# Two pairs of batch 2 move from TensorE to an elementwise local attention, and block 2's steps are reordered

## The chip, the cores and the metric

The kernel runs on one core of one Trainium2 chip. The metric is the device time of one execution in microseconds (us), the median of several runs; one further execution was taken by the hardware profiler. The engines are PE (TensorE, matrix products, with its weight loads counted apart as PEld), DVE (VectorE), ACT (ScalarE), POOL (GpSimd) and SP (SyncE, which here issues all DMAs). Each engine works through its own instructions strictly in order and waits on semaphores for the others. SBUF is the working memory with 128 partitions, PSUM the memory of 8 banks into which PE writes.

## The reference

The input q, k, v has 8 batches, 8 heads, 576 positions and 64 values per head. Two attentions are added and go through a feed-forward layer:

```python
q_d = q.reshape(B, H, Sd, 4, D).mean(axis=3)        # k_d, v_d alike; Sd = 144
out_up = np.repeat(sm_attn(q_d, k_d, v_d), 4, axis=2)
mask = np.abs(pos[:, None] - pos[None, :]) < 4       # 7 neighbours
attn = softmax(np.where(mask, scale * q @ k.T, -1e9))
x = (out_up + attn @ v).transpose(0, 2, 1, 3).reshape(B * S, H * D)   # 4608 x 512
r = np.maximum(x @ w_in, 0.0)                        # w_in 512 x 2048
out = (s * (r * r) + b) @ w_out                      # w_out 2048 x 512
```

All of it is float32.

## The kernel before

**Feed-forward.** The 4608 tokens are cut into 18 blocks of 256 (index t), and the 2048 hidden values into 8 f pairs of 256 (index p). A step (t, p) has a `gemm1` (lines 551 to 570: 24 matmuls into a PSUM tile `ph`, then relu, square and a rounded copy `gh` on ACT and the rest `gl` on DVE) and a `gemm2` (lines 586 to 616: 12 matmuls that add to two PSUM banks `po` of the block; at p = 7 the sums are scaled, given the bias and written out). Each float32 product is made from three products of rounded halves (lines 556 to 558 and 601 to 603). `gemm2` runs two or three steps behind `gemm1`, by the list `pend`. For t = 0 and t = 2 the tile `ph` is bank 4; t = 1 uses bank 7 up to p = 6 and bank 4 at p = 7; from t = 3 on, banks 4 and 6 take turns.

**Order of the steps** (lines 653 to 656): f pairs 0 to 6 for blocks 0 and 1 in turn, then f pairs 0 to 6 of block 2, then f pair 7 of blocks 0, 1 and 2, then block after block. The weights are converted meanwhile (`split_w`, lines 214 to 253): for f pairs 0 to 6 from staging tiles of 1024 elements, for f pair 7 from quarters of 256 (`load_quarter`, line 205), which are loaded into the tag `pv` with two buffers. The scratch tile `es` of this conversion is taken from `pv` for f pairs 0, 1 and 7, and from the tags `xl2` and `os` for the others. `add_rows` (line 572) adds the rows of w_out into `bias` on DVE, one f pair at each step from step 13 on, f pair 7 first; `column_sums` (line 581) makes the constant part of the output from it.

**Attention.** A unit is one pair of heads of one batch (pairs 0 to 3). The pooled attention (`down`, lines 268 to 342) uses PE, ACT, DVE and POOL alike in all units. The local attention has two forms. Batches 0, 1 and 2 (`first_unit`, lines 344 to 437) make scores in windows of 32 on PE (lines 383 and 388), a softmax on DVE and ACT, and the output again on PE (line 431). From batch 3 on, two pairs make a group (`local_unit`, lines 452 to 505): for each of 7 offsets POOL multiplies q by the shifted k (line 466) and DVE sums over the 64 values (468); after the softmax, for each offset DVE weights the shifted v (484, 487) and POOL or DVE adds (488). Nine transposes on PE (line 498) turn the sums, and DVE adds them into x (502). The scores `st` of a group stand in PSUM bank 7. `two_pairs` (line 511) weaves a group with the two pooled attentions that belong to it.

**Order of the attention.** `attention_rest` (line 664) yields a sequence of small pieces; after each step, `advance` emits pieces until a target is reached that grows for each batch from 0 at step `free[b]` to all its pieces (`NY[b]`) at step `need[b]`. The framework then orders each engine's instructions by priority and by a simulated timeline, so that pieces may run earlier or later than the step that emits them. `rings` gives the PSUM banks that the pieces of a batch take in turn: 5 and 6 for batch 1, 5 for the first two units of batch 2, and 2, 3 and 5 after that.

**Splits and buffers.** Before block t starts, `split_x` (line 529) needs the whole of the batches that it touches, and splits x into `xh` and `xl`; for block 2 in the tags `os` and `xl2` with one buffer each, for the others in `xh` and `xl` with two. Block 2 holds the end of batch 0 and the start of batch 1; block 4 the end of batch 1 and the start of batch 2. The output rows `os_` of every block stand in the tag `os`. The group's q and k (`lqk`) and v (`lv`) use the tags `big` and `vw`, one buffer each, which the units of `first_unit` use for `db` and `tvw`.

Of the kernel before, what the change touches and what calls it, by code (L numbers as in the profile page):

```python
# [11 lines left out]
F32 = mybir.dt.float32  # L12
F32R = mybir.dt.float32r
I32 = mybir.dt.int32
# [5 lines left out]
P = 128  # L20
B, H, S, D = 8, 8, 576, 64
HP = H // 2
FAC = 4
SD = S // FAC
DM = H * D
# [11 lines left out]
TB = 256  # L37
NB = NT // TB
NFP = DFF // 256
NK = DM // P  # L40
NE = 3
EU = NE * HP
CH = 9
NC_ = S // CH
HALO = FAC - 1
NO = 2 * HALO + 1
# [2 lines left out]

STAGE = (6, 6, 7, 6, 7, 6, 7)  # L50
CONVERT_AT = (1, 2, 4, 6, 7, 8, 11)
CHUNK = (512, 512, 512, 1024, 1024, 512, 1024)
BEHIND = {1: 400, 2: 100, 4: 100, 5: 400}
HF = 7
GROUPS = [(i // HP, i % HP // 2) for i in range(EU, B * HP, 2)]
# [7 lines left out]
def attention_ffn_kernel(ctx, tc, qk, vw_in, vr_in, vdm, qkn, vn, w_in, w_out, s_in, b_in, out):  # L63
    nc = tc.nc
# [3 lines left out]
    one = ctx.enter_context(tc.tile_pool(name="one", bufs=1))  # L68
    two = ctx.enter_context(tc.tile_pool(name="two", bufs=2))
    ps = ctx.enter_context(tc.tile_pool(name="ps", bufs=1, space=PS))  # L70

    def bank(i, shape, name):
        return ps.tile(shape, F32, tag=f"k{i}", name=name)
# [128 lines left out]
            nc.sync.dma_start(st.rearrange("p (k f) t -> p k (f t)", k=src.shape[1]), src)  # L202
            wst[(p, op)] = st

    def load_quarter(p, op, i):
        if op == "i":
            src = src_i[:, i, 512 * p : 512 * p + 512]
        else:
            src = src_o[:, 2 * p + i // 2, 512 * (i % 2) : 512 * (i % 2) + 512]
        st = two.tile([P, 256, 2], I32, tag="pv", name="wst")  # L210
        nc.sync.dma_start(st.rearrange("p f t -> p (f t)"), src)
        return st

    def convert(st, hi, lo, op, p):


        n = hi.shape[1]
        top, low = st[:, :, 1], st[:, :, 0]
        if p in (0, 1, 7):
            f = two.tile([P, n], F32, tag="pv", name="es")  # L220
        else:
            f = one.tile([P, n], F32, tag="xl2" if op == "i" else "os", name="es")
        w = f.bitcast(I32)


        nc.scalar.mul(f, top.bitcast(F32), 2.0 ** -112)
        nc.vector.tensor_scalar(f, f, W_MAX, -W_MAX, ALU.min, ALU.max)
        nc.vector.tensor_scalar(w, w, 3, 0x7FFFFFF8, ALU.logical_shift_left, ALU.bitwise_and)
        nc.vector.scalar_tensor_tensor(w, low, 29, w, ALU.logical_shift_right, ALU.bitwise_or)
        nc.vector.scalar_tensor_tensor(w, top, -0x80000000, w, ALU.bitwise_and, ALU.bitwise_or)  # L230
        nc.scalar.copy(hi, f)
        for i in range(0, n, 512):
            js = slice(i, min(i + 512, n))
            nc.vector.tensor_tensor(lo[:, js], f[:, js], hi.bitcast(F32)[:, js], ALU.subtract)
# [5 lines left out]
    def split_parts(p):  # L240
        wi[p] = one.tile([P, 2, NK, 256], F32R, tag=f"wi{p}", name="wi")
        wo[p] = one.tile([P, 2, 2, DM], F32R, tag=f"wo{p}", name="wo")
        for op, w in (("i", wi[p]), ("o", wo[p])):
            fl = w.rearrange("p s k f -> p s (k f)")
            if p < len(STAGE):
                st = wst.pop((p, op))
                for j in range(0, 1024, CHUNK[p]):
                    js = slice(j, j + CHUNK[p])
                    convert(st[:, js], fl[:, 0, js], fl[:, 1, js], op, p)
            else:  # L250
                for i in range(4):
                    cs = slice(256 * i, 256 * i + 256)
                    convert(load_quarter(p, op, i), fl[:, 0, cs], fl[:, 1, cs], op, p)


    xt = {}
# [195 lines left out]
    def local_unit(b, g, banks):  # L452

        acc = two.tile([P, CH, 2, D], F32, tag="qk", name="acc")

        st = bank(7, [P, 2, P], "st")
        for h in range(2):
            lqk = one.tile([P, 2 * CH + 2 * HALO, D], F32, tag="big", name="lqk")
            nc.sync.dma_start(lqk, qkn[GROUPS.index((b, g)), h])
            lv = one.tile([P, CH + 2 * HALO, D], F32, tag="vw", name="lv")  # L460
            nc.sync.dma_start(lv, vn[GROUPS.index((b, g)), h])
            ls = take(st[:, h], 0, [P, CH, NO])
            sums = st[:, h, 64 : 64 + CH]
            for o in range(NO):
                pr = two.tile([P, CH, D], F32, tag="pl", name="pr")
                nc.gpsimd.tensor_tensor(  # L466
                    pr, lqk[:, 0:CH], lqk[:, CH + o : 2 * CH + o], ALU.mult)
                nc.vector.tensor_reduce(ls[:, :, o], pr, AX.X, ALU.add)  # L468
                yield
            row = lambda t: t.unsqueeze(2).to_broadcast([P, CH, NO])  # L470
            nc.vector.tensor_tensor(ls, ls, omask, ALU.add)
            lr = two.tile([P, 2, CH], F32, tag="lr", name="lr")
            nc.vector.tensor_reduce(lr[:, 0], ls, AX.X, ALU.max)
            nc.vector.tensor_tensor(ls, ls, row(lr[:, 0]), ALU.subtract)
            nc.scalar.activation(ls, ls, AF.Exp, scale=SCALE)
            nc.vector.tensor_reduce(sums, ls, AX.X, ALU.add)
            nc.vector.tensor_scalar(sums, sums, 1e-9, None, ALU.add)
            nc.vector.reciprocal(lr[:, 1], sums)
            nc.vector.tensor_tensor(ls, ls, row(lr[:, 1]), ALU.mult)
            yield  # L480
            for o in range(NO):
                w = ls[:, :, o : o + 1].to_broadcast([P, CH, D])
                if o == 0:
                    nc.vector.tensor_tensor(acc[:, :, h], lv[:, 0:CH], w, ALU.mult)
                else:
                    pv = two.tile([P, CH, D], F32, tag="pv", name="pv")
                    nc.vector.tensor_tensor(pv, lv[:, o : o + CH], w, ALU.mult)  # L487
                    (nc.vector if o % 3 == 1 else nc.gpsimd).tensor_tensor(  # L488
                        acc[:, :, h], acc[:, :, h], pv, ALU.add)
                yield  # L490
        yield "ready"
        x = xt[b]
        for i0 in range(0, CH, 4):
            n = min(4, CH - i0)
            ot = banks([P, n, P], "ot")
            with tc.high_priority():
                for j in range(n):
                    nc.tensor.transpose(
                        ot[:, j], acc[:, i0 + j].rearrange("p h d -> p (h d)"), ident)
            for u in range(2):  # L500
                xv = x[:, 2 * g + u].rearrange("p (c i) -> p c i", i=CH)[:, :, i0 : i0 + n]
                nc.vector.tensor_tensor(
                    xv, ot[:, :, 64 * u : 64 * u + 64].rearrange("p j c -> p c j"), xv, ALU.add)
            yield
        complete.update((b, 2 * g + u) for u in range(2))
# [5 lines left out]
    def two_pairs(b, g, banks):  # L511
        for u in range(2):
            load_pair(b, 2 * g + u)
        dn = chain(*(down_unit(b, 2 * g + u, banks) for u in range(2)))
        lo = local_unit(b, g, banks)
        i = 0
        for said in lo:
            if said == "ready":
                for _ in dn:
                    yield  # L520
            elif i % 3 == 2:
                next(dn, None)
            i += 1
            yield
# [22 lines left out]

    gt = {}
    oacc = {}

    def gemm1(t, p):
        xh, xl = xs[t]
# [33 lines left out]
    def gemm2(t, p):  # L586
# [5 lines left out]
            oacc[t] = [bank(i, [P, DM], "po") for i in ob]  # L592
        po = oacc[t]
        end = t == NB - 1 and p == NFP - 1
        os_ = one.tile([P, 2, DM], F32, tag="os", name="os") if p == NFP - 1 else None
        for m in range(2):
            ms = slice(P * m, P * m + P)
            for j in range(2):
# [22 lines left out]
    def banks(*ids):  # L621
        ring = itertools.cycle(ids)
        return lambda shape, name: bank(next(ring), shape, name)
# [2 lines left out]
        for j in range(i, min(i + 3, EU)):  # L626
            load_pair(*units[j])

    NY = [10 * HP] * NE + [34 * (HP // 2)] * (B - NE)
    for hp in range(2, HP):  # L630
        load_pair(0, hp)
    load_w(0)
# [18 lines left out]


    order = [(t, p) for p in range(HF) for t in range(2)]
    order += [(2, p) for p in range(HF)]
    order += [(t, p) for p in range(HF, NFP) for t in range(3)]
    order += [(t, p) for t in range(3, NB) for p in range(NFP)]

    need = [0, 2 * HF - 3] + [(S * b // TB) * NFP - 3 for b in range(2, B)]
    free = [0, 0, 16] + [((S * (b - 1) - 1) // TB) * NFP - 2 for b in range(3, B)]


    rings = {1: banks(5, 6), 2: banks(5), 3: banks(2, 3, 5)}

    def attention_rest():
        for i in range(HP, EU):
            load_ahead(i)
            yield from first_unit(*units[i], rings[min(i // HP + i // (EU - 2), 3)])
        for b, g in GROUPS:
            yield from two_pairs(b, g, rings[3])

    gen = attention_rest()
    done = 0
    pend = []

    def target(st):
        return sum(
            min(1.0, max(0.0, (st - free[b]) / (need[b] - free[b]))) * NY[b]
            for b in range(1, B))

    def advance(st):  # L680
        nonlocal done
# [88 lines left out]
```

## Time and profile before

| what | us |
|---|---|
| median of 3 runs | 974.49 |
| lowest and highest of them | 971.71, 974.57 |
| the profiled execution | 972.49 |
| its span, first to last instruction | 970.7 |

The profile counts the share of the span in which an engine is busy; the ends of matmuls are modelled, so PE's share is too high where matmuls follow each other closely. The granted PE clock is 1.00 in the mean of the span. A row of the groups of instructions gives line, engine, operation, output and inputs with their shapes and the count, then the busy time and the mean duration in ns, then the idle time just ahead of them on their engine and what ended it. A row of the timeline gives start and duration in us; rows that follow each other on one line are merged. A row of the windows gives a stretch, then the busy time of PE, PEld, DVE, ACT and POOL in it with the count of instructions, the granted clock, the share of the DMA engines and GB/s.

### The profile page before, as it was taken

The page shows a single profiled execution, that of the slowest core. Times are in us where ns is not written, and L with a number is a line of the kernel's source. Part 1 is how long each engine was busy: PE and PEld are TensorE (multiplying, and loading weights), DVE is VectorE, ACT ScalarE, POOL GpSimd, SP SyncE. Part 2 cuts the span into 40 slices and gives each one's busy share as a digit, 9 for nine tenths or more (in the row PEclk, how much of TensorE's full clock was granted, in tenths as well). Part 3 has the DMA queues.
Part 4 walks back from the last instruction along what each step waited for, and adds up shares of the span by engine and source line. Part 5 has one row for each costly group of instructions (what it writes and reads, how often), then busy time and mean ns, then how long its engine had stood idle before and what let it go on. Part 6 is the DMA issues. An engine that isn't in the chain of part 4 may idle for free.

```text
span 970.7 us, 18541 instructions
## 1 busy us (share of the span) xinstructions
PE 938.7 (97%) x7316; PEld 843.4 (87%) x7316; DVE 637.7 (66%) x1175; ACT 475.0 (49%) x1141; POOL 418.0 (43%) x455
## 2 busy tenths in 40 slices
PE   5769999999999999999999999999999999999998
PEld 4559988888999999998888899989899999998987
DVE  5999996864567878787787878787878521211121
ACT  5878775553754453545363545453635433333231
POOL 9421011101066686776868786867676200000000
PEclk9999999999999999999999999999999999999999
DMA  9736512112243232323241424242412000000000
GB/s 316 261 121 210 172 60 78 49 42 73 101 134 113 77 110 72 102 70 133 67 136 66 135 68 131 72 134 69 136 55 76 1 22 1 23 1 22 1 23 22
DMA packets 32103, 86.26 MB, mean 89 GB/s; under 512 B 3344, under 2 KB 7952, under 8 KB 32016
## 3 DMA queue, kind: packets, MB, share of 16 engines
q1 hardware_dynamic: 32016, 85.08, 26.6%
q8 instruction: 57, 0.93, 0.4%
q14 instruction: 30, 0.25, 0.1%
HBM read 75.63 MB, written 9.44 MB: 88 GB/s over the span
## 4 chain that ended last, share of the span: by engine, by line
PE 74%; DVE 9%; DMA 8%; POOL 5%; ACT 2%; issue 2%; SPq 0%; DVEq 0%; ACTq 0%; POOLq 0%
PE ph L556 11%; PE ph L557 11%; PE ph L558 11%; PE po L603 11%; PE po L601 11%; PE po L602 11%; DMA tqk<-in_qk_dram 3%; POOL pr L466 3%; POOL acc L488 3%; DMA wst<-in_moe_w_out_dram 2%; PE sa L303 2%; DVE bias L579 1%; PE up L339 1%; PE ol L431 1%; DMA lqk<-in_qkn_dram 1%
## 5 line engine op out<-in xcount | busy, mean ns | idle before, releaser
L556 PE MATMUL ph<-xh,wi 128*128 128x256 f32 x1152 | 325.4, 283 | 3.7 <-ACT xh L542 2.5
L557 PE MATMUL ph<-xl,wi 128*128 128x256 f32 x1152 | 323.9, 281 | 0.0
L558 PE MATMUL ph<-xh,wi 128*128 128x256 f32 x1152 | 323.6, 281 | 0.0
L466 POOL TENSOR_TENSOR pr<-lqk 128x576 f32<-128x576 f32 x140 | 201.2, 1461 | 73.2 <-DMA lqk<-in_qkn_dram 29.2
L556 PEld LDWEIGHTS ph<-xh,wi 128*128 128x128 f32 x1152 | 217.5, 189 | 11.2 <-ACT xh L542 2.8
L557 PEld LDWEIGHTS ph<-xl,wi 128*128 128x128 f32 x1152 | 217.4, 189 | 5.4 <-issue 0.2
L558 PEld LDWEIGHTS ph<-xh,wi 128*128 128x128 f32 x1152 | 217.6, 189 | 0.3
L566 ACT ACTIVATE ph<-ph 128x512 f32<-128x512 f32 x144 | 83.8, 582 | 229.0 <-PE ph L558 223.2
L601 PE MATMUL po<-wo,gh 128*128 128x512 f32 x456 | 180.7, 396 | 0.0
L602 PE MATMUL po<-wo,gh 128*128 128x512 f32 x456 | 180.5, 396 | 0.0
L603 PE MATMUL po<-wo,gl 128*128 128x512 f32 x456 | 177.9, 397 | 0.0
L569 DVE TENSOR_TENSOR gl<-ph,gh 128x512 fp32r<-128x512 f32 x114 | 77.8, 683 | 115.8 <-ACT gh L568 115.5
L488 POOL TENSOR_TENSOR acc<-acc,pv 128x576 f32<-128x576 f32 x80 | 114.4, 1430 | 57.1 <-DVE acc L488 29.5
L468 DVE TENSOR_REDUCE st<-pr 128x9 f32<-128x576 f32 x140 | 105.9, 757 | 37.7 <-POOL pr L466 35.4
L292 POOL TENSOR_TENSOR dq<-vq 64x64 f32<-64x64 f32 x58 | 22.8, 393 | 197.4 <-PE up L337 195.3
L603 PEld LDWEIGHTS po<-wo,gl 128*128 128x128 f32 x456 | 85.7, 188 | 17.6 <-issue 0.2
L487 DVE TENSOR_TENSOR pv<-lv,st 128x576 f32<-128x576 f32 x120 | 87.5, 747 | 18.8 <-POOL acc L488 18.4
L601 PEld LDWEIGHTS po<-wo,gh 128*128 128x128 f32 x456 | 85.7, 188 | 15.9 <-ACT gh L568 0.6
L602 PEld LDWEIGHTS po<-wo,gh 128*128 128x128 f32 x456 | 85.7, 188 | 15.8
L568 ACT CAST gh<-ph 128x512 fp32r<-128x512 f32 x114 | 66.9, 587 | 64.3 <-PE po L602 62.4
L567 ACT ACTIVATE ph<-ph 128x512 f32<-128x512 f32 x144 | 83.7, 582 | 3.2
L602 PE MATMUL po<-wo,gb 128*128 128x512 f32 x120 | 47.1, 392 | 0.0
(149 smaller groups left out, 1239.3 us busy)
## 6 DMA issues: line engine op xcount, KB each, us to landing
tqk<-in_qk_dram SPq DMA_DIRECT2D x30, 584.0 KB, 4.1
lqk<-in_qkn_dram SPq DMA_DIRECT2D x20, 768.0 KB, 4.2
lv<-in_vn_dram SPq DMA_DIRECT2D x20, 480.0 KB, 3.4
out_dram<-os SPq DMA_DIRECT2D x17, 512.0 KB, 3.1
wst<-in_moe_w_in_dram SPq DMA_DIRECT2D x7, 1024.0 KB, 6.5
wst<-in_moe_w_out_dram SPq DMA_DIRECT2D x7, 1024.0 KB, 5.3
tvd<-in_vdm_dram SPq DMA_DIRECT2D x29, 160.0 KB, 2.9
tvr<-in_vr_dram SPq DMA_DIRECT2D x29, 128.0 KB, 3.1
```

Of the source, the lines that this page charges most:

```text
L466: nc.gpsimd.tensor_tensor(pr, lqk[:, 0:CH], lqk[:, CH + o : 2 * CH + o], ALU.mult)
L468: nc.vector.tensor_reduce(ls[:, :, o], pr, AX.X, ALU.add)
L487: nc.vector.tensor_tensor(pv, lv[:, o : o + CH], w, ALU.mult)
L488: (nc.vector if o % 3 == 1 else nc.gpsimd).tensor_tensor(acc[:, :, h], acc[:, :, h], pv, ALU.add)
L556: nc.tensor.matmul(ph[:, j], wi[p][:, 0, k, f], xh[:, k], start=(k == 0), stop=False)
L557: nc.tensor.matmul(ph[:, j], wi[p][:, 0, k, f], xl[:, k], start=False, stop=False)
L558: nc.tensor.matmul(ph[:, j], wi[p][:, 1, k, f], xh[:, k], start=False, stop=(k == NK - 1))
L566: nc.scalar.activation(ph, ph, AF.Relu)
L567: nc.scalar.activation(ph, ph, AF.Square)
L601: nc.tensor.matmul(po[m], gh[:, j, ms], wo[p][:, 0, j], start=first, stop=False)
L602: nc.tensor.matmul(po[m], gh[:, j, ms], wo[p][:, 1, j], start=False, stop=False)
L603: nc.tensor.matmul(po[m], gl[:, j, ms], wo[p][:, 0, j], start=False, stop=last)
```

## The change

- `EU` is 10 instead of 12: pairs 2 and 3 of batch 2 leave `first_unit` and become one group of `local_unit`, with its loads. For this group alone the scores `st` stand in SBUF, in the tag `ups`, since bank 7 belongs to block 2's sums by then. All of batch 2 uses bank 5 alone.
- The weights of f pair 7 are loaded by halves of 512 into the tags `os` and `xl2` (`load_half`), with the scratch tiles still in `pv`. F pair 6 takes its scratch tiles from `pv` as well, and converts in pieces of 512 instead of 1024.
- Block 2 starts after step 13 as before, but (0,7) and (1,7) stand between its f pairs 3 and 4 (steps 18 and 19, 21 and 22 before). The output rows of blocks 0 and 1 take one buffer each of the tags `xh` and `xl`.
- The targets: units 0 and 1 of batch 2 are emitted from step 13 to 16 (before, all of batch 2 from 16 to 29), the group from 16 to 27.

```diff
@@ -38,8 +38,7 @@
 NB = NT // TB
 NFP = DFF // 256
 NK = DM // P
-NE = 3
-EU = NE * HP
+EU = 10
 CH = 9
 NC_ = S // CH
 HALO = FAC - 1
@@ -49,7 +48,7 @@
 
 STAGE = (6, 6, 7, 6, 7, 6, 7)
 CONVERT_AT = (1, 2, 4, 6, 7, 8, 11)
-CHUNK = (512, 512, 512, 1024, 1024, 512, 1024)
+CHUNK = (512, 512, 512, 1024, 1024, 512, 512)
 BEHIND = {1: 400, 2: 100, 4: 100, 5: 400}
 HF = 7
 GROUPS = [(i // HP, i % HP // 2) for i in range(EU, B * HP, 2)]
@@ -202,13 +201,12 @@
             nc.sync.dma_start(st.rearrange("p (k f) t -> p k (f t)", k=src.shape[1]), src)
             wst[(p, op)] = st
 
-    def load_quarter(p, op, i):
-        if op == "i":
-            src = src_i[:, i, 512 * p : 512 * p + 512]
-        else:
-            src = src_o[:, 2 * p + i // 2, 512 * (i % 2) : 512 * (i % 2) + 512]
-        st = two.tile([P, 256, 2], I32, tag="pv", name="wst")
-        nc.sync.dma_start(st.rearrange("p f t -> p (f t)"), src)
+    def load_half(p, op, i):
+
+        src = src_i[:, 2 * i : 2 * i + 2, 512 * p : 512 * p + 512] if op == "i" else src_o[:, 2 * p + i]
+        st = one.tile([P, 512, 2], I32, tag=("os", "xl2")[i], name="wst")
+        to = st.rearrange("p (k f) t -> p k (f t)", k=2) if op == "i" else st.rearrange("p f t -> p (f t)")
+        nc.sync.dma_start(to, src)
         return st
 
     def convert(st, hi, lo, op, p):
@@ -216,7 +214,7 @@
 
         n = hi.shape[1]
         top, low = st[:, :, 1], st[:, :, 0]
-        if p in (0, 1, 7):
+        if p in (0, 1, 6, 7):
             f = two.tile([P, n], F32, tag="pv", name="es")
         else:
             f = one.tile([P, n], F32, tag="xl2" if op == "i" else "os", name="es")
@@ -248,9 +246,9 @@
                     js = slice(j, j + CHUNK[p])
                     convert(st[:, js], fl[:, 0, js], fl[:, 1, js], op, p)
             else:
-                for i in range(4):
-                    cs = slice(256 * i, 256 * i + 256)
-                    convert(load_quarter(p, op, i), fl[:, 0, cs], fl[:, 1, cs], op, p)
+                for i in range(2):
+                    cs = slice(512 * i, 512 * i + 512)
+                    convert(load_half(p, op, i), fl[:, 0, cs], fl[:, 1, cs], op, p)
 
 
     xt = {}
@@ -453,14 +451,19 @@
 
         acc = two.tile([P, CH, 2, D], F32, tag="qk", name="acc")
 
-        st = bank(7, [P, 2, P], "st")
+
+        n = CH * (NO + 1)
+        if b == 2:
+            st = one.tile([P, 2, n], F32, tag="ups", name="st")
+        else:
+            st = bank(7, [P, 2, n], "st")
         for h in range(2):
             lqk = one.tile([P, 2 * CH + 2 * HALO, D], F32, tag="big", name="lqk")
             nc.sync.dma_start(lqk, qkn[GROUPS.index((b, g)), h])
             lv = one.tile([P, CH + 2 * HALO, D], F32, tag="vw", name="lv")
             nc.sync.dma_start(lv, vn[GROUPS.index((b, g)), h])
             ls = take(st[:, h], 0, [P, CH, NO])
-            sums = st[:, h, 64 : 64 + CH]
+            sums = st[:, h, CH * NO : n]
             for o in range(NO):
                 pr = two.tile([P, CH, D], F32, tag="pl", name="pr")
                 nc.gpsimd.tensor_tensor(
@@ -547,6 +550,7 @@
 
     gt = {}
     oacc = {}
+    rows = []
 
     def gemm1(t, p):
         xh, xl = xs[t]
@@ -592,7 +596,10 @@
             oacc[t] = [bank(i, [P, DM], "po") for i in ob]
         po = oacc[t]
         end = t == NB - 1 and p == NFP - 1
-        os_ = one.tile([P, 2, DM], F32, tag="os", name="os") if p == NFP - 1 else None
+        if (t, p) == (0, NFP - 1):
+            rows.extend(two.tile([P, 2, DM], F32, tag=tag, name="os") for tag in ("xh", "xl"))
+        if p == NFP - 1:
+            os_ = rows[t] if t < 2 else one.tile([P, 2, DM], F32, tag="os", name="os")
         for m in range(2):
             ms = slice(P * m, P * m + P)
             for j in range(2):
@@ -626,7 +633,9 @@
         for j in range(i, min(i + 3, EU)):
             load_pair(*units[j])
 
-    NY = [10 * HP] * NE + [34 * (HP // 2)] * (B - NE)
+
+    ny = [10 * min(max(EU - HP * b, 0), HP) for b in range(B)]
+    NY = [n + 34 * ((HP - n // 10) // 2) for n in ny]
     for hp in range(2, HP):
         load_pair(0, hp)
     load_w(0)
@@ -651,31 +660,34 @@
 
 
     order = [(t, p) for p in range(HF) for t in range(2)]
-    order += [(2, p) for p in range(HF)]
-    order += [(t, p) for p in range(HF, NFP) for t in range(3)]
+    rest = iter((2, p) for p in range(NFP))
+    order += [next(rest) if t == "2" else (int(t), NFP - 1) for t in "2222012222"]
     order += [(t, p) for t in range(3, NB) for p in range(NFP)]
 
     need = [0, 2 * HF - 3] + [(S * b // TB) * NFP - 3 for b in range(2, B)]
-    free = [0, 0, 16] + [((S * (b - 1) - 1) // TB) * NFP - 2 for b in range(3, B)]
-
-
-    rings = {1: banks(5, 6), 2: banks(5), 3: banks(2, 3, 5)}
+    need[2] -= 2
+    free = [0, 0, 13] + [((S * (b - 1) - 1) // TB) * NFP - 2 for b in range(3, B)]
+
+
+    rings = {1: banks(5, 6), 2: banks(5)}
+    late = banks(2, 3, 5)
 
     def attention_rest():
         for i in range(HP, EU):
             load_ahead(i)
-            yield from first_unit(*units[i], rings[min(i // HP + i // (EU - 2), 3)])
+            yield from first_unit(*units[i], rings[i // HP])
         for b, g in GROUPS:
-            yield from two_pairs(b, g, rings[3])
+            yield from two_pairs(b, g, rings.get(b, late))
 
     gen = attention_rest()
     done = 0
     pend = []
 
+    spans = [(free[b], need[b], NY[b]) for b in range(1, B) if b != 2]
+    spans += [(free[2], 16, ny[2]), (16, need[2], NY[2] - ny[2])]
+
     def target(st):
-        return sum(
-            min(1.0, max(0.0, (st - free[b]) / (need[b] - free[b]))) * NY[b]
-            for b in range(1, B))
+        return sum(min(1.0, max(0.0, (st - lo) / (hi - lo))) * n for lo, hi, n in spans)
 
     def advance(st):
         nonlocal done
```

## The prediction

> **What bounds the kernel now.** I read the page first: its busy times, then its slices.
>
> ```profile
> span 970.7 us, 18541 instructions
> PE 938.7 (97%) x7316; PEld 843.4 (87%) x7316; DVE 637.7 (66%) x1175; ACT 475.0 (49%) x1141; POOL 418.0 (43%) x455
> ```
>
> 97% busy could still hide waits, since the ends of matmuls are modelled. So the next view is the list of waits, for PE alone, from 70 us (its feed-forward matmuls have just begun) to 967 us (they are done).
>
> ```profile
> PE sl L383 <- DVE pl L394: 1.1, 1, 1.1
> PE ph L556 <- DVE gb L569: 1.0, 2, 0.6
> PE ot L498 <- POOL acc L488: 1.0, 1, 1.0
> PE sl L383 <- ACT pd L307: 0.5, 1, 0.5
> PE ph L556 <- DVE gl L569: 0.2, 1, 0.2
> ```
>
> Each row gives the waiting instruction, what it waited for, the total, the count and the longest: 3.8 us of waiting in almost 900 us. So from 70 us on the time is what stands in PE's queue, and an operation taken off PE there is worth its slot on PE (from its start to the start of what follows), as long as no other engine comes late in its place. Gains on DVE, POOL or the DMA queues are worth nothing by themselves.
>
> **What the change takes off PE.** Two units, pairs 2 and 3 of batch 2, lose their local scores (lines 383 and 388) and their outputs (431). Their nearest relative is the last of these units before the change, in PE's timeline:
>
> ```profile
> 252.77 0.28 PE L557 MATMUL ph<-xl,wi 128*128 128x256 f32 x1
> 252.98 1.26 PE L431 MATMUL ol<-db,tvw 128*64 128x96 f32 x24
> 254.17 0.38 PE L558 MATMUL ph<-xh,wi 128*128 128x256 f32 x1
> 254.39 0.28 PE L556 MATMUL ph<-xh,wi 128*128 128x256 f32 x1
> 254.51 0.28 PE L557 MATMUL ph<-xl,wi 128*128 128x256 f32 x1
> ...
> 256.97 0.26 PE L383 MATMUL sl<-maskb,idb 128*128 128x192 bf16 x1
> ...
> 257.72 0.79 PE L388 MATMUL sl<-tqk 64*32 64x32 f32 x68
> 258.44 0.38 PE L558 MATMUL ph<-xh,wi 128*128 128x256 f32 x1
> 258.66 0.29 PE L556 MATMUL ph<-xh,wi 128*128 128x256 f32 x1
> ```
>
> Starts are what counts here. The 24 output matmuls hold PE from 252.98 to 254.17, 1.19 us; the matmul ahead of them takes 0.21 to its successor and the one behind 0.22, where an undisturbed one takes 0.12 (254.39 to 254.51), another 0.19. The scores of both heads hold it from 256.97 to 258.44, 1.47 us, and the matmul behind them takes 0.10 too long. Together 2.95 us a unit, 5.9 us for two.
>
> **What it puts on PE.** One group of nine transposes (line 498), as batch 3's first group has them:
>
> ```profile
> 329.67 1.14 PE L498 MATMUL ot<-ident,acc 128*128 128x128 f32 x9
> 330.57 0.36 PE L558 MATMUL ph<-xh,wi 128*128 128x256 f32 x1
> 330.77 0.28 PE L556 MATMUL ph<-xh,wi 128*128 128x256 f32 x1
> ```
>
> 0.90 us, and 0.08 of disturbance behind it. In batch 2 they go through one PSUM bank instead of three, so the three pieces come apart and disturb PE three times: 1.2 us, and 1.0 to 1.4 as bounds. The matmuls of the pooled attention (scores, transposes, up) stay. Balance on PE: 1.2 - 5.9 = -4.7 us.
>
> **What it puts on the others.** The group costs, by the groups of instructions (busy, mean ns):
>
> ```profile
> L466 POOL TENSOR_TENSOR pr<-lqk 128x576 f32<-128x576 f32 x140 | 201.2, 1461 | 73.2 <-DMA lqk<-in_qkn_dram 29.2
> L468 DVE TENSOR_REDUCE st<-pr 128x9 f32<-128x576 f32 x140 | 105.9, 757 | 37.7 <-POOL pr L466 35.4
> L488 POOL TENSOR_TENSOR acc<-acc,pv 128x576 f32<-128x576 f32 x80 | 114.4, 1430 | 57.1 <-DVE acc L488 29.5
> L487 DVE TENSOR_TENSOR pv<-lv,st 128x576 f32<-128x576 f32 x120 | 87.5, 747 | 18.8 <-POOL acc L488 18.4
> ```
>
> POOL: 14 products and 8 sums, 14 x 1.461 + 8 x 1.430 = 31.9 us. DVE: 14 reductions and 14 weightings (the two of offset 0 taken at the same price), 14 x 0.757 + 14 x 0.747 = 21.1 us, and four sums. Whether there is room, the windows of the stage say (PE, PEld, DVE, ACT, POOL busy):
>
> ```profile
> 140.00:177.00 37.00, 36.02 (x323) 31.03 (x322) 23.25 (x60) 21.39 (x55) 2.52 (x6) 1.00 0.24 79
> 177.00:207.00 30.00, 29.40 (x334) 25.35 (x335) 29.07 (x52) 14.45 (x35) 4.47 (x6) 1.00 0.14 44
> 207.00:285.00 78.00, 77.82 (x750) 69.50 (x750) 38.20 (x72) 41.93 (x107) 18.06 (x27) 1.00 0.25 82
> ```
>
> From 207 to 285 us DVE is free for 39.8 us and POOL for 59.9; DMA is at a quarter. The group fits beside PE and I cost it at nothing there. Only 177 to 207 is full on DVE (29.07 of 30): this is where the 31 bias additions of `add_rows` stand. If the group's work lands there, it delays the `gl` subtractions that PE waits for; that is the first rival.
>
> **Scores in SBUF.** With `st` in SBUF, the group's weightings read both inputs from SBUF, as the bias additions do. Here are two runs of those on DVE, and what POOL did during the first:
>
> ```profile
> 185.84 5.89 DVE L579 TENSOR_TENSOR bias<-bias,wo 128x512 f32<-128x512 f32 x7
> 194.30 3.59 DVE L579 TENSOR_TENSOR bias<-bias,wo 128x512 f32<-128x512 f32 x5
> ...
> 185.82 1.60 POOL L292 TENSOR_TENSOR dq<-vq 64x64 f32<-64x64 f32 x2 [33.26 <-PE up L337]
> ```
>
> Alone, an addition takes 0.72 us (3.59 / 5); beside POOL 0.84 (5.89 / 7), and two POOL operations took 1.60. By this 17% the 14 weightings cost DVE some 1.8 us more, in cover, so nothing. [...]
>
> **Weights of f pair 7, by halves.** Now each quarter is loaded into the two-buffer tag from which its scratch tile also comes, so load and conversion alternate. The last conversion, and the split of block 2's x:
>
> ```profile
> 176.35 0.42 DVE L234 TENSOR_TENSOR wo<-es,wo 128x256 fp32r<-128x256 f32 x1 [0.20 <-ACT wo L231]
> ...
> 156.06 0.96 DVE L543 TENSOR_TENSOR xl<-x,xh 128x768 fp32r<-128x768 f32 x1 [0.20 <-ACT xh L542]
> ```
>
> Halves have two staging tiles of their own, so the second load runs under the first conversion. DVE has 13.8 free us in 140 to 177, and larger pieces cost less:
>
> ```profile
> L230 DVE SCALAR_TENSOR_TENSOR es<-wst,es 128x512 int32<-128x512 int32 x16 | 11.1, 702 | 0.0
> L230 DVE SCALAR_TENSOR_TENSOR es<-wst,es 128x256 int32<-128x256 int32 x8 | 3.4, 420 | 0.2
> ```
>
> 4 x 0.702 = 2.8 us instead of 8 x 0.420 = 3.4 for this one of five operations. I expect the last conversion near 160 us. By itself that gives PE nothing. It brings `add_rows` forward, and two waits of the first list (1.1 and 0.5, pairs of batch 2 in this DVE-full stretch) may go: between 0 and -1.6, taken as -0.8. f pair 6 now converts in pieces of 512 too: two more per operand kind, off PE's path, nothing. But the staging tiles have the tags `os` and `xl2`, where x of block 2 must go next: block 2's split now waits for the last conversion (the fourth rival).
>
> **The new order of steps** moves (0,7) and (1,7) three steps ahead, each with its matmuls, its output rows and the output DMA, which on SP now stands ahead of batch 2's later loads. The rows go into the freed `xh`/`xl`, so nothing waits for block 2. PE's work is the same: nothing. Pairs 0 and 1 of batch 2 come about three steps earlier, the same work.
>
> New waits are certain to be there in some number, since one `ph` bank serves blocks 2 and the two inserted steps. Bounds 0 and 4 us (priced in the first rival), taken as 1.0. **Sum:** -4.7 - 0.8 + 1.0 = -4.5 us. The profiled execution took 972.49 us (span 970.7), so it would become 968.0; the median of the three runs, 974.49, lies 2.0 above it, and becomes 970.0.
>
> **Rival 1: the holes were being filled.** While block 2 runs, each gemm1 must wait until relu, square, copy and subtraction have emptied the one `ph` bank:
>
> ```profile
> 162.90 0.28 PE L558 MATMUL ph<-xh,wi 128*128 128x256 f32 x1
> 169.57 0.28 PE L556 MATMUL ph<-xh,wi 128*128 128x256 f32 x1
> ```
>
> Between block 2's first two steps 6.7 us pass. PE filled them with gemm2 steps that it had in store and with attention matmuls. With 2.95 us of filling gone from each of two units, 5.9 us over the ten steps of that time, and the group's 0.75 us operations ahead of `gl` on DVE, I put 0.5 us of opened waiting on each of eight steps: 4 us, and the result is 974.5 - 4.7 + 4 = 973.8. For: DVE's full stretch. Against: the first list has 0.2 us of this wait, and the removed matmuls stood mostly behind this stretch.
>
> **Rival 2 (no gain in staging).** If the halves convert as late as now, 176 us, block 2's split comes 20 us later than 156.06. PE can cover 6.7 us with the gemm2 steps in store and some with pairs 0 and 1. I put the damage at 2 to 10 us: 972 to 980. For: DVE must now do the whole conversion before the split. Against: the 13.8 idle us.
>
> **Rival 3, slower: batch 2 is late for block 4.**
>
> ```profile
> 270.29 0.37 SPq L459 DMA_DIRECT2D lqk<-in_qkn_dram  x1
> 270.64 0.69 DVE L543 TENSOR_TENSOR xl<-x,xh 128x512 fp32r<-128x512 f32 x1 [0.26 <-ACT xh L542]
> 285.19 0.28 PE L556 MATMUL ph<-xh,wi 128*128 128x256 f32 x1
> ...
> 224.12 0.46 DVE L434 TENSOR_TENSOR x<-ol,ups 128x288 f32<-128x288 f32 x1 [3.11 <-PE ol L431]
> ```
>
> Batch 3's first group took 59.4 us from its load (270.29) to its last transposes (329.67), with the additions into x some 65 (my allowance for these). The group of batch 2 can load only when unit 1 of batch 2 has let go of `big`; the load waits in SP's queue and holds up every load behind it. Block 4's x (split at 270.64, used at 285.19) must be complete by about 285.19 - 4.7 - 1.5 = 279, with 1.5 for the split, twice the 0.69 of its subtraction. So the point is 279 - 65 = 214 us: a unit that ends later delays PE one for one. With free starting three steps earlier I expect 195 to 205. If it keeps its present end, 224.12, PE loses 10 us: 980. [...]
>
> **How the numbers follow.** Three runs spread over 0.3%, which is also about what a measurement of this kernel can tell from no change, 2.9 us. The forecast, 0.56: faster. Rival 1, 0.22: the same. Rival 2, 0.11, half the same, half slower. Rival 3, 0.11, of it 0.04 in the harsher form: slower. Faster 0.56; same 0.22 + 0.05 = 0.27; slower 0.06 + 0.11 = 0.17. Range: below, the sum with no new waits and both old ones gone, -6.3, gives 968.2, less the 2.8 by which the fastest run lies under the median: 965.5. Above, rival 1 and the milder half of the others: 976.5.
>
> **What would show it.** Right: 192 matmuls fewer on line 388 and 48 on 431; PE's waits after 70 us still under 6 us; the last f-pair conversion near 160; batch 2 complete before 275; every later block 4 to 5 us earlier and the end 4.5 earlier. Wrong: PE's list led by `ph` waiting for `gl` (rival 1), by `xh`/`xl` of block 2 near 160 (rival 2) or of block 4 near 280 (rival 3), or an unchanged start of block 4's first step.

## The result and the profile after

The changed kernel took 982.49 us (median of 4 runs, 982.22 to 984.79), the kernel before beside it 973.3 (4 runs, 971.71 to 974.57): a ratio of 1.011, with a 95% interval of 1.0094 to 1.0127. It is slower by about 1%, where 970.0 us and so a gain was forecast, and the time lies above the range of 965.5 to 976.5. The profiled execution took 982.63 us, with a span of 980.8, 10.1 over before.

The head of the page of the changed kernel, and its slices of granted PE clock:

```profile
span 980.8 us, 18094 instructions
PE 938.4 (96%) x7081; PEld 842.8 (86%) x7081; DVE 667.3 (68%) x1193; ACT 472.6 (48%) x1129; POOL 460.6 (47%) x477
...
PEclk9999999999898999999999999999999999999999
```

PE has 235 records fewer, but is busy for the same time: some of its work ran at a lower clock, 0.50 in two stretches of 6.8 us (windows below). The groups of PE by line show that the removal itself is as described (960 score and 216 output matmuls before):

```profile
L386 PE MATMUL sl<-tqk 64*32 64x32 f32 x768 | 13.0, 213 | 0.0
L429 PE MATMUL ol<-db,tvw 128*64 128x96 f32 x168 | 11.0, 287 | 3.7 <-ACT db L412 3.7
```

The list of PE's waits from 70 to 980 us, changed kernel:

```profile
PE tp L320 <- ACT pd L312: 3.3, 1, 3.3
PE tr L325 <- DVE x L505: 3.1, 1, 3.1
PE ph L560 <- DVE gl L573: 2.2, 3, 1.5
PE ot L501 <- POOL acc L491: 1.5, 1, 1.5
PE sl L381 <- DVE pl L392: 1.3, 1, 1.3
PE ph L561 <- DVE xl L546: 0.7, 1, 0.7
PE po L608 <- ACT gh L572: 0.5, 2, 0.3
PE ot L501 <- DVE x L505: 0.3, 1, 0.3
```

12.9 us instead of 3.8. The two longest stand alone, and before each of them ends the clock falls. Windows of the changed kernel (PE, PEld, DVE, ACT and POOL busy, then the granted clock); each pair goes from the last matmul's start ahead of the wait to the fall, and from there to the end of the half clock:

```profile
244.77:247.41 2.64, 0.39 (x2) 0.00 (x0) 2.61 (x6) 0.01 (x1) 1.82 (x2) 1.00 0.50 200
247.41:254.24 6.83, 5.76 (x24) 5.12 (x25) 6.83 (x10) 2.43 (x7) 6.02 (x3) 0.50 0.20 77
299.26:302.03 2.77, 0.30 (x1) 0.11 (x1) 2.47 (x4) 0.00 (x0) 2.77 (x3) 1.00 0.79 221
302.03:308.85 6.82, 5.51 (x24) 5.01 (x25) 6.46 (x10) 4.01 (x13) 5.30 (x4) 0.50 0.50 166
```

Each time the clock stays at half for 6.8 us, and the feed-forward matmuls in it follow each other at 0.21 us instead of 0.11. Half of PE's work there is lost, an estimate: 5.76 x 0.5 = 2.9 us behind the first wait, 5.51 x 0.5 = 2.8 behind the second, in sum 5.6. So the 10.1 us of span are: waits 12.9 - 3.8 = +9.1, half clock +5.6, and the removed matmuls, -4.7 by the prediction's price. That makes 10.0. The first feed-forward matmul also comes at 65.8 us instead of 64.6; whether these 1.2 us last to the end is not shown, and the sum does without them.

**Where the first wait comes from.** DVE and POOL of the changed kernel at 240 us, while batch 2's group computes its first softmax:

```profile
240.97 0.59 DVE L302 TENSOR_REDUCE dmx<-sa 96x3 f32<-96x432 f32 x1
241.48 2.55 DVE L480 TENSOR_SCALAR st<-st 128x9 f32<-128x9 f32 x1
243.95 0.74 DVE L471 TENSOR_REDUCE st<-pr 128x9 f32<-128x576 f32 x1
...
245.44 1.18 DVE L482 TENSOR_TENSOR st<-st,lr 128x63 f32<-128x63 f32 x1
...
247.21 0.16 DVE L310 RECIPROCAL dsm<-dsm 96x3 f32<-96x3 f32 x1
```

```profile
241.46 0.46 POOL L286 TENSOR_TENSOR vq<-tvr 128x128 f32<-128x128 f32 x1
241.88 0.74 POOL L285 TENSOR_TENSOR vt<-tvd 80x256 f32<-80x256 f32 x1
242.58 1.43 POOL L469 TENSOR_TENSOR pr<-lqk 128x576 f32<-128x576 f32 x1
```

An operation on nine values per partition (172 ns in the kernel before) takes 2.55 us: it begins 0.02 us behind the first of three POOL operations and ends with the last, at 244.0. The small product at 245.44 (230 ns in the kernel before) takes 1.18 us, and POOL computes another product from 244.77 to 246.54. Behind both in DVE's order stands the reciprocal `dsm` of the pooled attention, on which `pd` and so PE's `tp` wait until 248.5.

**Where the second comes from.** The group's transposes and their additions into x (PE, then DVE):

```profile
287.92 0.66 PE L501 MATMUL ot<-ident,acc 128*128 128x128 f32 x4 [1.54 <-POOL acc L491]
...
294.66 0.60 PE L501 MATMUL ot<-ident,acc 128*128 128x128 f32 x4
...
299.26 0.30 PE L501 MATMUL ot<-ident,acc 128*128 128x128 f32 x1 [0.28 <-DVE x L505]
302.64 0.66 PE L325 MATMUL tr<-ident,pd 96*64 96x96 f32 x3 [3.08 <-DVE x L505]
303.20 0.80 PE L560 MATMUL ph<-xh,wi 128*128 128x256 f32 x2
```

```profile
292.43 0.75 DVE L505 TENSOR_TENSOR x<-ot,x 128x256 f32<-128x256 f32 x2
...
298.37 0.74 DVE L505 TENSOR_TENSOR x<-ot,x 128x256 f32<-128x256 f32 x2
...
302.06 0.43 DVE L505 TENSOR_TENSOR x<-ot,x 128x64 f32<-128x64 f32 x2
```

Three pieces go through one PSUM bank: the next transposes wait until DVE, busy with batch 3's group, has emptied it. 15 us pass from the first piece to the last, and block 4's first step starts at 303.20 instead of 285.19. PE spent the time until then on other steps in store, so most of the 18 us were not lost.

### The profile page after: what moved, and what is told of

Read it like the earlier page. It is cut to its first block, busy times and chain, and to the rows that moved or that the text cites. A ratio compares the mean times of both kernels' runs of the same rounds, so it can differ in the third digit from the quotient of the medians.

```text
span 980.8 us, 18094 instructions
## 1 busy us (share of the span) xinstructions
PE 938.4 (96%) x7081; PEld 842.8 (86%) x7081; DVE 667.3 (68%) x1193; ACT 472.6 (48%) x1129; POOL 460.6 (47%) x477
## 4 chain that ended last, share of the span: by engine, by line
PE 83%; DVE 6%; POOL 4%; DMA 4%; ACT 1%; issue 1%; SPq 0%; DVEq 0%; POOLq 0%
PE ph L560 13%; PE ph L561 13%; PE ph L562 13%; PE po L608 12%; PE po L609 12%; PE po L610 12%; PE sa L301 2%; POOL pr L469 2%; PE up L337 1%; DMA flat<-in_vr_dram 1%; POOL acc L491 1%; PE ol L429 1%; PE ot L501 1%; DVE pv L490 1%; DMA tvr<-in_vr_dram 1%
## 5 line engine op out<-in xcount | busy, mean ns | idle before, releaser
L469 POOL TENSOR_TENSOR pr<-lqk 128x576 f32<-128x576 f32 x154 | 220.8, 1458 | 82.1 <-DMA lqk<-in_qkn_dram 56.0
L562 PEld LDWEIGHTS ph<-xh,wi 128*128 128x128 f32 x1152 | 218.9, 190 | 0.5 <-issue 0.2
L491 POOL TENSOR_TENSOR acc<-acc,pv 128x576 f32<-128x576 f32 x88 | 128.2, 1457 | 56.3 <-DVE acc L491 32.6
L471 DVE TENSOR_REDUCE st<-pr 128x9 f32<-128x576 f32 x154 | 116.4, 756 | 37.3 <-POOL pr L469 34.9
L490 DVE TENSOR_TENSOR pv<-lv,st 128x576 f32<-128x576 f32 x132 | 99.2, 774 | 14.7 <-POOL acc L491 14.2
L290 POOL TENSOR_TENSOR dq<-vq 64x64 f32<-64x64 f32 x58 | 28.6, 493 | 149.2 <-PE up L335 147.0
```

The source lines that it names most:

```text
L469: nc.gpsimd.tensor_tensor(pr, lqk[:, 0:CH], lqk[:, CH + o : 2 * CH + o], ALU.mult)
L491: (nc.vector if o % 3 == 1 else nc.gpsimd).tensor_tensor(acc[:, :, h], acc[:, :, h], pv, ALU.add)
L562: nc.tensor.matmul(ph[:, j], wi[p][:, 1, k, f], xh[:, k], start=False, stop=(k == NK - 1))
```

## The experiments

There are five candidates for the loss. L: batch 2's group loads late (218.51, when unit 1 lets go of `big`). P: the scores in SBUF set DVE and POOL against each other. B5: the ring of one bank. B3: batch 3's work stands between batch 2's. O: order and staging cost time by themselves. Each kernel's diff is against the one named and shows the lines that matter, not all. All ratios are to the kernel before, measured beside each run; its medians there were 972.0 to 972.4 us.

**1. Order and staging without the move** (against the changed kernel):

```diff
-EU = 10
+EU = 12
-    need[2] -= 2
-    free = [0, 0, 13] + ...
+    free = [0, 0, 16] + ...
-    rings = {1: banks(5, 6), 2: banks(5)}
+    rings = {1: banks(5, 6), 2: banks(5), 3: late}
```

> The changed kernel without the move: all four units of batch 2 keep their scores and outputs on TensorE (EU 12, batch 2's targets and banks as before); the new order of steps, the staging by halves and the output rows stay. Theory L (batch 2's group is late for block 4, because it can load only when `big` is let go, and then takes over 80 us): the loss disappears, 970 to 975 us, and block 4's first step starts near 285 us. Theory O (the new order with one ph bank, or the staging, costs the time): it stays near 980 to 983.

979.27 us, ratio 1.0072 (1.0057 to 1.0087). So order and staging together cost 6.9 us with all twelve units in place, and L can't be the only cause.

**2. The move without order and staging** (order, staging and rows of the kernel before):

> The kernel before with the move alone (scores of this group in SBUF, bank 5 alone and the new targets for batch 2), old order of steps, old staging by quarters. Theory L: the loss stays or grows, 980 to 990 us, since the units of batch 2 end no earlier. Theory O: the gain of 4.7 us on TensorE shows, 967 to 972.

1006.84 us, 1.0357 (1.0326 to 1.0388), 24 us over the changed kernel: in this form (scores in SBUF, one bank, early emission) the move does far worse without the other two parts. The head of this run's list of PE's waits:

```profile
PE ph L559 <- DVE gl L572: 18.8, 13, 2.9
PE ph L559 <- DVE os L616: 8.0, 1, 8.0
```

The feed-forward matmuls wait for DVE, where the group's work stands among the subtractions `gl`, and once for the output rows.

**3. Batch 3 emitted four steps later** (`free[3] += 4`, against the changed kernel):

> The changed kernel with batch 3's pieces emitted from step 34 on instead of 30, so that none of them stands between the last pieces of batch 2's group. Theory B3 (the group takes 84 us instead of 65 because GpSimd and VectorE work on batch 3 between its pieces): the group ends 10 to 15 us earlier, block 4 starts near 290 us, 973 to 977 in all. If the interleaving only uses gaps: 980 to 985, or later blocks lose what block 4 gains.

983.18 us, 1.0109 (1.0085 to 1.0133), and batch 3's products stand between batch 2's as before: the framework's own ordering decides that, not the step that emits them. This tells nothing for or against B3, which stays open.

**4. Three banks for batch 2's group**, emitted from step 20 (against the changed kernel):

```diff
-            yield from two_pairs(b, g, rings.get(b, late))
+            yield from two_pairs(b, g, late)
-    spans += [(free[2], 16, ny[2]), (16, need[2], NY[2] - ny[2])]
+    spans += [(free[2], 16, ny[2]), (20, need[2], NY[2] - ny[2])]
```

> The changed kernel with banks 2, 3 and 5 instead of 5 alone for batch 2's group, whose pieces are emitted from step 20 on (banks 2 and 3 are block 1's until then). Theory B5 (the one bank holds up the group's pooled attention and its last transposes): the waits of a transpose for VectorE's additions (3.1 us) and for ScalarE's exponentials (3.3 us) go, with them one dip of the granted clock, 974 to 978. If the group is late by its loads and its elementwise work alone: 980 to 983.

976.74 us (972.23 to 980.58), 1.005 (1.0026 to 1.0074): 5.7 us of the loss gone, with a wide spread. The run changes the banks and the emission at once; run 12 parts them.

**5. Scores in PSUM** (bank 5; the group's other tiles in banks 2 and 3, emitted from step 20.5; against the changed kernel):

```diff
-        if b == 2:
-            st = one.tile([P, 2, n], F32, tag="ups", name="st")
-        else:
-            st = bank(7, [P, 2, n], "st")
+        st = bank(5 if b == 2 else 7, [P, 2, n], "st")
```

> The changed kernel, with the scores of batch 2's group in PSUM (bank 5) and its other tiles in banks 2 and 3, emitted from step 20.5. Against the run with the three banks (976.7 us, scores in SBUF) only the place of the scores and one bank of the ring differ. Theory P (the scores in SBUF put DVE's elementwise steps and POOL's in each other's way, and the group is stretched by it): a weighting goes from some 1.05 us back to about 0.75, a POOL sum from 1.9 to about 1.45, the group from 73 us to about 63, it ends some 8 us earlier, and the time is 970 to 974 us. Theory B5 (the single bank alone made the group late) and theory O (what is left over the kernel before is the order of the steps): the group may be shorter, but the time stays within 975 to 978 us.

976.0 us, 1.0036 (1.0022 to 1.0049). The weightings are back at 746 ns (row below), but the time is that of run 4.

**6. The kernel before with all ten groups' scores in SBUF:**

```diff
-        st = bank(7, [P, 2, P], "st")
+        st = one.tile([P, 2, CH * (NO + 1)], F32, tag="ups", name="st")
```

> The kernel before with the scores of all its ten groups in SBUF instead of PSUM bank 7, nothing else. Theory P: in every group a weighting takes about 1.05 us for 0.75 and the small steps up to several times as long, a group lasts some 8 us longer than the 61 us of before, and those that end close to their block's start put PE behind: 976 to 990 us. Rival (the slow steps of the changed kernel came from its crowded stretch, not from the place of the scores): weightings stay at about 0.75 us and the time within 0.3% of before, 970 to 976 us.

1056.57 us, 1.0877 (1.0856 to 1.0899): 84 us for ten groups. The groups of DVE by form from 200 to 960 us, first of this run, then of the kernel before:

```profile
L487 DVE TENSOR_TENSOR pv<-lv,st 128x576 f32<-128x576 f32 x120 | 128.2, 1087 | 12.2 <-POOL acc L488 11.7
L471 DVE TENSOR_TENSOR st<-st,omask 128x63 f32<-128x63 f32 x20 | 21.7, 1084 | 0.3
```

```profile
L471 DVE TENSOR_TENSOR st<-st,omask 128x63 f32<-128x63 f32 x20 | 4.5, 225 | 0.4
```

The weighting goes from 747 ns (the prediction's row) to 1087, the small mask addition from 225 to 1084. P is a real price: 8.4 us a group when every group pays it. What follows from late groups is in it, PE's waits and its clock (58 us of this trace stand at 0.50).

**7. The order alone, 8. the staging alone** (each added to the kernel before):

> The kernel before with the new order of the steps alone (the last steps of blocks 0 and 1 between block 2's, their rows in the tiles xh and xl); twelve units, staging by quarters. The run with order and staging, without the move, was at 979.3 us, 6.9 us over before. Theory O1 (the order costs it: the attention's matmuls of batch 2 fall between more matmuls of the blocks and take 86 us of PE for 79): 977 to 981 us. Rival O2 (the staging by halves costs it, as block 2 is split later): 971 to 975 us.

> The kernel before with the staging of the last f pair by halves alone; twelve units, the old order of the steps. Theory O1 (the order costs the 6.9 us): 971 to 975 us, with the last conversion some 15 us earlier than before and nothing made of it. Rival O2 (the staging costs it, since its halves lie in the tiles that block 2's split needs and hold that back from 156 to about 165 us): 976 to 981 us.

Order: 971.5 us, 0.9988 (0.9976 to 1.0). Staging: 977.51, 1.0059 (1.0037 to 1.0082). The order costs nothing; the halves cost 5.3 us, the opposite of what O1 and my prediction had. In all these runs "the halves" take with them f pair 6's smaller pieces and its scratch tiles in `pv`; the two were not tried apart. PE of the staging run, scores of a unit of batch 2:

```profile
168.78 0.26 PE L381 MATMUL sl<-maskb,idb 128*128 128x192 bf16 x1
168.97 0.62 PE L386 MATMUL sl<-tqk 64*32 64x32 f32 x48
170.91 0.26 PE L381 MATMUL sl<-maskb,idb 128*128 128x192 bf16 x1 [1.32 <-DVE pl L392]
...
171.72 0.79 PE L605 MATMUL po<-wo,gh 128*128 128x512 f32 x1
```

Both heads' scores stand back to back in one bank, with nothing between to fill the wait: 2.94 us, where the prediction's row had 1.47. These 2.94 us hold the wait of 1.32, and right behind it this trace has 3.4 us at half clock (171.5 to 174.9). From the step ahead of block 2's first (152 us in both kernels) to the seventh step after it, the attention's matmuls take 11.7 us of PE from start to start (280 matmuls) instead of 8.2 (268). Block 2's split comes at 164 and not 156 us. It waits for the last unit of batch 1:

```profile
161.19 1.21 PE L429 MATMUL ol<-db,tvw 128*64 128x96 f32 x24
162.70 0.84 ACT L545 CAST xh<-x 128x768 fp32r<-128x768 f32 x1 [3.04 <-DVE x L432]
```

Before, that unit's output matmuls began at 152.15. Here the steps of its softmax stand on DVE between the conversions of the halves. Whether this makes it late, and whether it is the whole price, was not tried.

**9. Order and move without the halves** (run 5 with quarters), **10. the changed kernel with quarters:**

```diff
-                for i in range(2):
-                    cs = slice(512 * i, 512 * i + 512)
-                    convert(load_half(p, op, i), ...)
+                for i in range(4):
+                    cs = slice(256 * i, 256 * i + 256)
+                    convert(load_quarter(p, op, i), ...)
```

> The run with the scores of batch 2's group in PSUM (976.0 us), with the last f pair staged by quarters as in the kernel before: so the new order and the move, without the halves. Theory A (the parts add up: the order alone was at -0.7 us, the halves alone at +5.3, and the move with its scores in PSUM at -3.3, the difference of 976.0 to the 979.3 of order and halves): 967 to 970 us, under both kernels. Theory B (the halves are needed for the move: the quarters hold DVE's and POOL's work until 176 us, and so batch 2's units and its group): 973 to 977 us.

> The changed kernel with the last f pair staged by quarters as in the kernel before, nothing else: the new order, and the move with the scores in SBUF and the one bank. Theory A (the parts add up): 982.5 less the 5 to 7 us that the halves cost, 975 to 978 us, still over before. Theory B (the halves bring the move its time): 983 us or more, since the units and the group of batch 2 come later.

Run 9: 971.75 us, 0.9995 (0.9984 to 1.0006), the best form of the move, and no faster than before. Run 10: 989.77, 1.0173 (1.0154 to 1.0192). So the halves cost 4.3 us (976.0 to 971.75) where the group has two banks and PSUM scores, and bring 7.3 where it has neither. Run 7's and 8's prices add up for the first kernel and fail for the second; why the halves help there is not settled.

**11. Scores back in SBUF** in run 5, nothing else:

> The run with the scores in PSUM (976.0 us) with the scores put back in SBUF and nothing else: banks 2 and 3 for the group's other tiles, emitted from step 20.5. Theory P (the place of the scores stretches the group, as it did by 8.4 us for each of the ten groups in the kernel before with SBUF scores): the weightings go from 0.75 to about 1.0 us, the group ends 6 to 10 us later, and the time is 979 to 985 us. Theory B5 (what was lost was lost to the one bank): 975 to 978 us, as the run with three banks.

977.58 us, 1.0051 (1.0033 to 1.0069): 1.6 us over run 5, and the intervals overlap. DVE by form from 222 to 291 us, run 5 and then run 11:

```profile
L487 DVE TENSOR_TENSOR pv<-lv,st 128x576 f32<-128x576 f32 x13 | 9.5, 746 | 1.1 <-POOL acc L488 0.9
```

```profile
L490 DVE TENSOR_TENSOR pv<-lv,st 128x576 f32<-128x576 f32 x12 | 18.3, 1541 | 0.7 <-POOL acc L491 0.7
```

The weightings take twice as long, 9 us of DVE more, but from its first product to its last addition the group takes 69 us instead of 65, and little of that reaches the end. P acts, and is not what cost most here.

**12. One bank, emitted from step 20.5:** run 11 with the ring of one bank, or the changed kernel with the later emission.

> The changed kernel with batch 2's group emitted from step 20.5 instead of 16, bank 5 alone as it has it. The run with banks 2 and 3 (977.6 us) differs from this one in the ring alone, and from the changed kernel (982.5 us) in ring and emission. Theory B5 (the ring of one bank costs the 4.9 us): 981 to 984 us, with the group's transposes in three turns some 3 to 6 us apart. Rival E (the early emission costs them, as it ranks the group's work ahead of block 2's): 976 to 979 us, with the transposes still in three turns.

985.57 us, 1.0145 (1.0128 to 1.0162). The transposes of run 12 and then those of run 11:

```profile
289.46 1.05 PE L501 MATMUL ot<-ident,acc 128*128 128x128 f32 x4
297.82 0.60 PE L501 MATMUL ot<-ident,acc 128*128 128x128 f32 x4
302.57 0.30 PE L501 MATMUL ot<-ident,acc 128*128 128x128 f32 x1 [0.90 <-DVE x L505]
305.56 0.66 PE L325 MATMUL tr<-ident,pd 96*64 96x96 f32 x3 [2.69 <-DVE x L505]
```

```profile
285.93 1.09 PE L501 MATMUL ot<-ident,acc 128*128 128x128 f32 x8 [0.61 <-POOL acc L491]
289.89 0.27 PE L501 MATMUL ot<-ident,acc 128*128 128x128 f32 x1
```

With two banks the transposes are through in 4 us, with one in 13. B5 is shown: 8.0 us for the one bank (bank 5, which units 0 and 1 of batch 2 use as well) instead of two. Rival E falls, since the early emission gives 3.1 us back.

Read as a chain, each run differs from the one above in one thing. The last column is an estimate like the one above: half of PE's busy time at a clock of 0.50 in the run's trace, from 75 us on.

| kernel | us | step | lost at half clock |
|---|---|---|---|
| before | 972.2 | | 0 |
| new order | 971.5 | -0.7 | 0 |
| and the move: scores in PSUM, two banks | 971.75 | +0.3 | 0 |
| and the halves | 976.0 | +4.3 | 3.4 |
| and the scores in SBUF | 977.6 | +1.6 | 1.7 |
| and one bank | 985.6 | +8.0 | 8.1 |
| and early emission: the changed kernel | 982.5 | -3.1 | 5.6 |

By this estimate most of the two large steps is clock: 3.4 of the 4.3 us of the halves and 6.4 of the 8.0 of the bank. The waits ahead of it can be short; in run 5's trace the clock falls at 173.3 and 292.7 us, beside two waits of 1.3 us (171.0 to 172.3, 291.4 to 292.7). It is not the halves' whole price, though: run 1 has them, is 6.9 us late and has no half clock from 75 us on.

## Why the prediction was wrong

- **The removed matmuls (-4.7).** They are gone, but no run got the whole gain: the move is +0.3 us in run 9, and -3.3 beside the halves (run 5 against run 1). Run 9's list of waits says where it went:

```profile
PE ph L558 <- DVE gl L571: 2.9, 4, 1.3
PE ph L559 <- DVE xl L544: 1.3, 1, 1.3
PE po L606 <- ACT gh L570: 1.2, 3, 0.7
PE ot L499 <- DVE x L503: 0.8, 1, 0.8
PE sa L302 <- DVE x L503: 0.7, 1, 0.7
PE tr L326 <- ACT ptm L328: 0.2, 1, 0.2
```

  7.1 us, where the order alone has 2.8 (1.2, 0.8, 0.5 and 0.3): 4.3 us of new waits take the place of 4.7 us of work. `ot`, `sa` and `xl` among them stand at block 4's start, 290.9 us. So "worth its slot as long as no other engine comes late in its place" was right as a rule, and its condition failed.
- **"The group fits beside PE and I cost it at nothing there": the step that failed.** I compared sums of busy time with free time, and a chain of 22 alternating steps of two engines doesn't fit by its sum. The third rival's 65 us were met with two banks and scores in PSUM (run 5: 65 us from the first product to the last addition). The changed kernel took 79.5 (223.0 to 302.5) and run 12 took 84, so batch 2 was complete at 302.5 where the prediction asked for 275. In place of nothing the runs showed 9.1 us of new waits and some 5.6 of half clock behind them.
- **The one bank.** I priced it at three disturbances of PE's transposes, 1.2 us. It holds the group and the pooled attention of the same batch in one queue behind DVE, and cost 8.0.
- **Scores in SBUF.** By the 17% row I had 1.8 us on DVE, in cover. Weightings went up by 40% in the changed kernel's crowded stretch (1046 ns on average from 244 to 289 us), by 106% in run 11 (1541 ns, beside 746 with the scores in PSUM in run 5). In the same stretches the reductions, of one input, stayed at 745 and 746 ns. The bias additions were a poor stand-in: POOL did only 1.60 us of work beside their 5.89, but 54.2 us in the 69 us of run 11's stretch (222 to 291 us).
- **Unit 1 of batch 2 at 195 to 205 us.** It ended at 218.9, 5.7 us ahead of before. The two units still end 27.8 us apart in the one bank (191.1 and 218.9; before 30.2, 194.4 and 224.6), and emitting them three steps earlier does little to that distance. With the third rival's point of 214 this alone says 5 us late.
- **Halves of f pair 7.** The last conversion came at 157.9 us, as expected near 160, and cost 4 to 5 us instead of bringing 0.8: an earlier end off the path was worth nothing. Block 2's split came at 165.0 instead of 156.06, but behind batch 1's last unit (its additions into x at 163.09 and 164.06) and not behind the staging tiles, as the second rival (once called the fourth) had it.
- **The new order: nothing.** Right, by run 7.

The third rival, at 0.11, is what happened in kind: batch 2 late for block 4, its load at 218.51. It lacked the ring and the clock behind the waits. No run shows what the 0.04 for its harsher form rests on; with the scores in SBUF the runs showed weightings of 1541 ns for 746 and POOL's sums at 1494 ns for 1433 (runs 11 and 5, 222 to 291 us). Two small things: the lower bound comes to 965.4 and not 965.5, and the base of 974.49 lay 2 us above the 972.0 to 972.4 that the kernel before took beside the later runs. Neither changes the sign.

## What to carry to other kernels

Work moved from the bound engine to two others is paid by its chain and its buffers, not by their free time: lay the chain out from its load to its due time, with every bank and buffer that it shares, and compare the lengths. Put what DVE weights by into PSUM when GpSimd works beside it (746 ns a weighting here, for 1541 in SBUF), and don't give a late chain a ring of one. A change of several parts is best tried as a chain of kernels that each differ in one: here the best form of the move gained nothing, and the rest cost over 10 us. Count the clock as well as the waits: in the staging run 3.4 us at half clock, some 1.7 us of lost work by estimate, stand behind a wait of 1.3.

## What the runs showed of the hardware

A DVE operation on 9 values per partition, of one input, took 2.55 us in the changed kernel (from 241.48 us) for 0.17 in the kernel before. It ended with the third of three POOL operations in a row, though the second and the third began after it, at 241.88 and 242.58 us. Run 3's trace has the same at the same place (238.82 us, 2.55 us). What held it is not shown; the reductions, also of one input, took 745 ns (changed kernel, 244 to 289 us) and 757 in the kernel before.

The clock of PE is 1.00 in the changed kernel from 75 us to the end of the work, but for two stretches at 0.50 of 6.83 us each (247.41 to 254.24, 302.03 to 308.85); the kernel before has none (1.00 from 75 to 970 us). The clock fell 2.64 and 2.77 us after the last matmul's start (244.77 to 247.41, 299.26 to 302.03), ahead of the end of waits of 3.3 and 3.1 us. In run 12 it fell at 288.4, where the feed-forward matmuls go from 0.12 us apart to 0.21, when PE had been at work again for 1.3 us after a wait of 2.2. In the changed kernel the half clock added some 2.9 and 2.8 us, the estimate above, to the two waits of 3.3 and 3.1 us.
